# Units of 64 queries instead of 32 in a banded attention, with the global keys apart and the turns moved to transposing transfers

## The chip, the cores and the metric

The kernel runs on one core of one Trainium2 chip. The time is device microseconds of the whole launch. The core has five engines that run their own instruction streams and meet only at semaphores: TensorE (PE; its weight loads are listed apart as PEld), VectorE (DVE), ScalarE (ACT), GpSimdE (POOL) and SyncE (SP). Transfers are carried by 16 DMA engines; here POOL's queue brings the inputs in, and SP's queue moves data within the chip's memory, turns it, and stores the output. PE reads operands from the on-chip memory of 128 partitions and writes to PSUM, which has eight banks of 512 float32 a partition; all eight are in use.

## What is computed

There are 8 batches of 8 heads, 512 local and 32 global tokens each, with a head dimension of 64. A global query attends to all 544 tokens. A local query attends to the 32 global tokens and to the local ones at most 32 positions away. The result, 4352 rows of 512, goes through two matrices of 512 x 2048 and 2048 x 512 with a hard-swish between them ("MoE" in the names, though there is one expert).

```python
window = 32
s_g   = scale * q_g @ concat(k_g, k_l).T          # global queries: everything
out_g = softmax(s_g) @ concat(v_g, v_l)
s_ll  = where(|i - j| <= window, scale * q_l @ k_l.T, -1e9)
s_lg  = scale * q_l @ k_g.T
out_l = softmax(concat(s_lg, s_ll)) @ concat(v_g, v_l)
x = concat(out_g, out_l)                          # (4352, 512)
h = x @ w_in
out = (h * clip(h + 3, 0, 6) / 6) @ w_out
```

## The kernel before

**Work of one tile.** For each batch b and each j of 0 to 3, `local_step` handles 128 queries of all 8 heads.

- Score (L741, L748): the 128 queries are cut into 4 units of 32. A unit sees 96 local keys, so the score of a head is 32 global columns and 96 local ones, 128 in all. The global part takes 8 matmuls of a full 128*128 array with 32 columns (L741; `kgz` holds the global keys of a head pair with zeros for the other head). The local part takes 32 matmuls on pieces of 64*32 of the array, 96 columns each (L748). All 8 heads fill two PSUM banks, `s`.
- Softmax: per head, DVE adds the mask, scales, takes the extreme (L763) and ACT takes the exponential with its sum (L774). DVE then takes reciprocals (L785) and scales in two halves (L789) into `pn`, 8 x 128 columns of float16.
- Turn: `pn` is turned into `et`, keys on the partitions. In batches 0 to 3 PE does it (L797) by 8 transposing matmuls into the bank `t`, and DVE or ACT copies that out; from batch 4 on (`TURN_E = 4`) SP issues a transposing transfer (L808).
- AV (L830): 16 matmuls of a full array with 64 columns, each for one unit and two heads. Their weights are V "strips" in `st`: for every unit, 32 rows of global V and 96 rows of local V on one set of partitions. Seven SP transfers a batch build them (`strips_moved`, L624). Batch 0 (`NEAR = 1`) does without strips and uses 6 groups of smaller pieces instead (`av_near`, L822).
- Evacuation: two copies of 64 partitions each (L410 on ACT, L412 on DVE) from the banks `a` to `xt`, the second after the first.

**Other steps.** Loads of q and k are turned to `qk` by PE (L677) up to batch 4 and by a transfer (L667) from batch 5 on (`TURN_QK = 5`). The global queries of a batch take one score (L865, 64*32 pieces, in the banks of `s` and `a` together), a softmax into two `pg` of 640 columns, two turns of five matmuls on PE (L904), and an AV of 20 matmuls (L918). The MoE part is `first` (L941, matmuls into one of three banks `m`, ACT L948, DVE L952) and `second` (L964, an evacuation, and a store by SP, L981). Its matmuls have 512 columns, except in batches 0 and 1, where `first` works on 128 or 256 tokens at a time.

**What sets the order.** Nothing is scheduled on the chip. A planner in the kernel (`Plan.lay`) holds every step with its engine, an assumed duration and a sort key, and lays them out in time, with rings of buffers and a model of the two DMA queues; `RANKS` shifts the key of single steps. The instructions are issued in the order of the planned starts, and each engine runs its own list strictly in that order. Up to batch 1's first AV (`NEAR` before, 1 after), the planner also puts filler matmuls (L1093) into planned gaps of PE, which keep it busy.

Of the kernel before, what the change touches and what calls it, by code (L numbers as in the profile page):

```python
# [8 lines left out]
FP32 = mybir.dt.float32  # L9
# [13 lines left out]
    ('first', 0, 0, 0): -5.75, ('first', 0, 0, 1): 0.67, ('first', 0, 0, 2): 0.4, ('first', 0, 0, 3): 6.76,  # L23
    ('first', 0, 1, 0): 0.4, ('first', 0, 1, 1): 1.43, ('first', 0, 1, 2): -4.6, ('first', 0, 1, 3): -0.17,
    ('first', 0, 2, 0): -0.94, ('first', 0, 2, 1): -0.54, ('first', 0, 2, 2): -20.75, ('first', 0, 2, 3): -5.21,
    ('first', 1, 0, 0): -1.01, ('first', 1, 0, 1): -23.76, ('first', 1, 0, 2): -0.6, ('first', 1, 0, 3): 0.03,
    ('first', 1, 1, 0): 0.85, ('first', 1, 1, 2): -0.63, ('first', 1, 1, 3): 21.84, ('first', 2, 0, 0): -17.92,
    ('first', 2, 0, 1): 0.44, ('first', 2, 0, 2): -21.92, ('first', 2, 0, 3): 0.52, ('first', 3, 0, 1): 0.09,
    ('first', 3, 0, 2): -0.07, ('first', 3, 0, 3): 0.03, ('first', 4, 0, 0): -27.07, ('first', 4, 0, 1): -13.96,
    ('first', 4, 0, 2): -38.28, ('first', 4, 0, 3): -23.15, ('first', 5, 0, 0): -12.9, ('first', 5, 0, 1): -13.16,  # L30
    ('first', 5, 0, 2): -2.15, ('first', 5, 0, 3): 0.54, ('first', 6, 0, 0): -20.42, ('first', 6, 0, 1): -21.28,
    ('first', 6, 0, 2): -0.07, ('first', 6, 0, 3): -18.08, ('first', 8, 0): 0.87, ('first', 8, 1): -0.2,
    ('first', 8, 2): -0.03, ('first', 8, 3): 1.73,
    ('gav', 0): -13.93, ('gav', 1): 12.35, ('gav', 2): 6.1, ('gav', 3): -1, ('gav', 4): 1.99, ('gav', 5): -7.53,
    ('gav', 6): 3.03, ('gav', 7): 3.5,
    ('gscore', 0): -0.3, ('gscore', 1): -0.5, ('gscore', 2): -2.91, ('gscore', 3): 0.71, ('gscore', 4): -0.1,
    ('gscore', 5): 2.75, ('gscore', 6): 13.26, ('gscore', 7): 25.36,
    ('gsoft', 0): -1.87, ('gsoft', 1): 1.47, ('gsoft', 2): 1.59, ('gsoft', 3): -1.64, ('gsoft', 4): 0.79,
    ('gsoft', 5): 1.77, ('gsoft', 7): -0.1,
    ('gturned', 0): -28.89, ('gturned', 1): -12.61, ('gturned', 2): -4.03, ('gturned', 3): -2.33,  # L40
    ('gturned', 4): 0.6, ('gturned', 5): 4.12, ('gturned', 6): 3.37, ('gturned', 7): -6.87,
    ('keys', 1): -1.63, ('keys', 2): -0.33, ('keys', 3): 5.83, ('keys', 4): -0.3, ('keys', 7): 3.91,
    ('load', 0, 'g'): 1.15, ('load', 0, 'h'): -0.15, ('load', 0, 'v', 0): 0.54, ('load', 0, 'v', 1): -0.1,
    ('load', 0, 'v', 2): 0.3, ('load', 0, 'v', 3): 0.76, ('load', 0, 'v', 4): 1.12, ('load', 0, 0, 0): -0.22,
    ('load', 0, 0, 1): -0.3, ('load', 0, 1, 0): 0.89, ('load', 0, 1, 1): 3.09, ('load', 0, 2): -0.06,
    ('load', 0, 3): 0.76, ('load', 1, 'v', 0): 3.07, ('load', 1, 'v', 1): 4.91, ('load', 1, 'v', 3): 3.42,
    ('load', 1, 'v', 4): 5.23, ('load', 1, 0): 1.79, ('load', 1, 1): 0.76, ('load', 1, 2): 1.79,
    ('load', 1, 3): 2.27, ('load', 2, 'g'): -0.2, ('load', 2, 'v', 0): 3.39, ('load', 2, 'v', 1): 2.09,
    ('load', 2, 'v', 2): 1.05, ('load', 2, 'v', 3): 0.37, ('load', 2, 'v', 4): 4.22, ('load', 2, 0): 3.39,
    ('load', 2, 1): 2.67, ('load', 2, 2): 1.54, ('load', 2, 3): -0.03, ('load', 3, 'v', 0): 2.17,  # L50
    ('load', 3, 'v', 1): 0.06, ('load', 3, 'v', 2): -0.97, ('load', 3, 'v', 3): 1, ('load', 3, 'v', 4): 4.07,
    ('load', 3, 0): 2.8, ('load', 3, 1): 1.41, ('load', 3, 2): 1.31, ('load', 3, 3): 2.5, ('load', 4, 'g'): 3.96,
    ('load', 4, 'v', 0): -2.18, ('load', 4, 'v', 1): -0.3, ('load', 4, 'v', 2): 2.86, ('load', 4, 'v', 3): 0.6,
    ('load', 4, 'v', 4): -1.81, ('load', 4, 0): 5.52, ('load', 4, 2): 1.29, ('load', 4, 3): 0.96,
    ('load', 5, 'v', 0): 4.13, ('load', 5, 'v', 1): 8.46, ('load', 5, 'v', 2): 12.41, ('load', 5, 'v', 3): 3.46,
    ('load', 5, 'v', 4): 4.75, ('load', 5, 0): 12.72, ('load', 5, 1): 17.91, ('load', 5, 2): 3.86,
    ('load', 5, 3): 7.2, ('load', 6, 'g'): 0.17, ('load', 6, 'v', 0): 0.64, ('load', 6, 'v', 1): 6.46,
    ('load', 6, 'v', 2): 15.64, ('load', 6, 'v', 3): 6.5, ('load', 6, 'v', 4): 5.97, ('load', 6, 0): 0.5,
    ('load', 6, 1): 47.7, ('load', 6, 2): 0.03, ('load', 6, 3): -6.89, ('load', 7, 'v', 0): -5.4,
    ('load', 7, 'v', 1): -3.6, ('load', 7, 'v', 2): -2.3, ('load', 7, 'v', 3): -9.19, ('load', 7, 'v', 4): -2.87,  # L60
    ('load', 7, 0): 24.13, ('load', 7, 1): 16.14, ('load', 7, 2): 24.5, ('load', 7, 3): 18.29,
    ('scale', 0, 0): -16.01, ('scale', 0, 1): -5.01, ('scale', 0, 2): 1.29, ('scale', 0, 3): -35.33,
    ('scale', 1, 0): -0.04, ('scale', 1, 1): 2.47, ('scale', 1, 2): -3.97, ('scale', 1, 3): 1.16,
    ('scale', 2, 0): 0.3, ('scale', 2, 1): -3.59, ('scale', 2, 2): -2.23, ('scale', 2, 3): -0.73,
    ('scale', 3, 0): 5.95, ('scale', 3, 1): -0.03, ('scale', 3, 2): -2.15, ('scale', 3, 3): -0.03,
    ('scale', 4, 0): -2.42, ('scale', 4, 1): 3.51, ('scale', 4, 2): 0.2, ('scale', 4, 3): 2.27,
    ('scale', 5, 0): 0.27, ('scale', 5, 1): -3.93, ('scale', 5, 2): -1.76, ('scale', 5, 3): -3.01,
    ('scale', 6, 0): -0.33, ('scale', 6, 1): 0.27, ('scale', 6, 2): 2.07, ('scale', 6, 3): 0.27,
    ('scale', 7, 0): 0.51, ('scale', 7, 1): -1.99, ('scale', 7, 2): 0.25, ('scale', 7, 3): 10.31,
    ('score', 0, 0): 5.87, ('score', 0, 1): -0.66, ('score', 0, 2): 3.85, ('score', 0, 3): 1.13,  # L70
    ('score', 1, 1): -0.27, ('score', 1, 2): -4.39, ('score', 1, 3): -0.3, ('score', 2, 0): -0.3,
    ('score', 2, 1): 2.89, ('score', 2, 2): 0.1, ('score', 2, 3): -12.27, ('score', 3, 0): 1.88,
    ('score', 3, 1): 1.72, ('score', 3, 2): 0.64, ('score', 3, 3): 9.74, ('score', 4, 0): -3.93,
    ('score', 4, 1): -4.05, ('score', 4, 2): 1.04, ('score', 4, 3): -0.71, ('score', 5, 0): -0.48,
    ('score', 5, 1): -0.3, ('score', 5, 2): 4.12, ('score', 5, 3): 1.41, ('score', 6, 0): -1.63,
    ('score', 6, 1): 13.99, ('score', 6, 2): 6.98, ('score', 6, 3): 9.74, ('score', 7, 0): 11.38,
    ('score', 7, 1): 16.28, ('score', 7, 2): 13.94, ('score', 7, 3): 16.91,
    ('second', 0, 0): 0.3, ('second', 0, 1): 0.08, ('second', 0, 2): -3.22, ('second', 0, 3): 0.08,
    ('second', 1, 0): -0.32, ('second', 1, 1): -1.02, ('second', 1, 2): 0.28, ('second', 1, 3): 1,
    ('second', 2, 0): 0.39, ('second', 2, 1): 0.69, ('second', 2, 2): 0.97, ('second', 2, 3): -0.76,  # L80
    ('second', 3, 0): -0.11, ('second', 3, 1): -0.43, ('second', 3, 2): 1.19, ('second', 3, 3): -0.27,
    ('second', 4, 0): 6.42, ('second', 4, 1): 7.47, ('second', 4, 2): 5.52, ('second', 4, 3): -0.13,
    ('second', 5, 0): 15.37, ('second', 5, 1): 11.1, ('second', 5, 2): 14.56, ('second', 5, 3): -1.03,
    ('second', 6, 0): 60.42, ('second', 6, 1): 28.72, ('second', 6, 2): 48.59, ('second', 6, 3): 13.46,
    ('second', 7, 0): 3.75, ('second', 7, 1): 38.92, ('second', 7, 2): 23.81, ('second', 7, 3): 30.25,
    ('second', 8, 0): 1.26, ('second', 8, 1): 2.54,
# [1044 lines left out]
```

## Time and profile before

| | |
|---|---|
| Median of 3 runs | 330.6 us (329.19 to 332.8) |
| Profiled execution | 330.47 us, its span 328.7 us |
| Granted PE clock, mean | 0.995 |
| Busy: PE, DVE, ACT, POOL | 317.9, 264.4, 249.1, 105.6 us |
| MoE matmuls L964 and L941, busy | 128.4 and 120.1 us |
| Fillers, L1093 | 28 |
| Turns of `et` and `qk` by transfer | 16 and 12, 4.9 us to land (median) |
| `st` strips, transfers per batch | 7 (384, 512, 256 and 128 KB) |

Matmuls are pipelined, so the lengths of single matmuls overlap, and busy PE is not PE at its peak. What a step costs is the distance from its first start to the start of what follows. The DMA share is the mean busy share of the 16 DMA engines in a stretch, and is above 1 where two queues have packets in flight on the same engine. Idle time of an engine that is not the bottleneck costs nothing.

### The profile page before, as it was taken

How to read it: one execution, taken by the hardware profiler on the slowest of the kernel's cores; microseconds unless marked ns; L12 is line 12 of the kernel's file. 1: busy time of each engine (PE TensorE's matmuls, PEld its weight loads, DVE VectorE, ACT ScalarE, POOL GpSimd, SP SyncE). 2: the span in 40 equal slices, each digit the busy share in tenths (PEclk: the TensorE clock that was granted, in tenths of full speed). 3: DMA queues.
4: the chain of work that ended last, by engine and by line, in shares of the span. 5: the costliest groups of instructions: out<-in, count | busy, mean ns of one | idle time of the engine just before them, and what ended most of it. 6: DMA issues, size and time to landing. Idle time of an engine off the chain costs nothing.

```text
span 328.7 us, 10251 instructions
## 1 busy us (share of the span) xinstructions
PE 317.9 (97%) x3892; PEld 190.7 (58%) x3892; DVE 264.4 (80%) x972; ACT 249.1 (76%) x787; POOL 105.6 (32%) x139
## 2 busy tenths in 40 slices
PE   8799899999999999999899999999999999999996
PEld 4478795678676555645445545554545545448453
DVE  6999999889979999898899799576987997377100
ACT  4789899879968889886888798587977894466121
POOL 8849626962870962137600500041000000000000
PEclk9979999999999999999999999999999999999999
DMA  9999999999999999399999999969753313100032
GB/s 161 174 190 171 197 281 176 159 200 235 194 155 245 178 206 203 47 136 190 205 191 253 165 224 201 198 106 183 185 130 98 35 27 103 59 7 0 3 97 96
DMA packets 152898, 49.83 MB, mean 152 GB/s; under 512 B 137936, under 2 KB 145936, under 8 KB 152848
## 3 DMA queue, kind: packets, MB, share of 16 engines
q0 software_dynamic: 106560, 17.05, 69.9%
q1 hardware_dynamic: 46288, 32.12, 42.5%
q8 instruction: 30, 0.49, 0.6%
q14 instruction: 20, 0.16, 0.1%
HBM read 35.19 MB, written 8.91 MB: 134 GB/s over the span
## 4 chain that ended last, share of the span: by engine, by line
PE 79%; DVE 10%; DMA 5%; ACT 3%; issue 1%; SPq 0%; ACTq 0%
PE m L964 34%; PE m L941 30%; PE a L830 4%; DVE sm L763 3%; DMA et<-pn 2%; PE s L748 2%; DVE gs L952 2%; PE t L797 2%; DMA st<-ve 2%; ACT sm L774 2%; PE a L822 1%; PE t L677 1%; PE s L741 1%; DMA st<-in_q_l_dram 1%; DVE pn L789 1%
## 5 line engine op out<-in xcount | busy, mean ns | idle before, releaser
L964 PE MATMUL m<-wout,gs 128*128 128x512 f16 (+1 forms) x560 | 128.4, 373 | 0.0
L941 PE MATMUL m<-xt,win 128*128 128x512 f16 (+2 forms) x704 | 120.1, 321 | 1.2 <-DVE gs L952 0.7
L774 ACT ACTIVATE sm<-sm,stat 128x128 f32<-128x128 f32 x256 | 100.0, 393 | 13.9 <-DVE stat L763 13.3
L952 DVE SCALAR_TENSOR_TENSOR gs<-t,m 128x512 f16<-128x512 f32 x136 | 91.0, 683 | 14.6 <-ACT t L948 13.9
L941 PEld LDWEIGHTS <-win 128*128 128x128 f16 x768 | 68.3, 98 | 47.9 <-issue 2.8
L948 ACT ACTIVATE t<-m 128x512 f32<-128x512 f32 x136 | 80.1, 594 | 19.8 <-PE m L941 18.9
L964 PEld LDWEIGHTS <-gs 128*128 128x128 f16 x560 | 51.2, 98 | 50.8 <-issue 1.1
L763 DVE CUSTOM_DVE_ANT_0 sm<-s,mask 128x128 f32<-128x128 f32 x256 | 60.0, 283 | 3.9 <-PE s L748 3.4
L774 ACT ACTIVATION_READ_ACCUMULATOR sm<-sm,stat 128x1 f32 x256 | 48.8, 191 | 0.0
L505 POOL DMA_DIRECT2D ve<-in_v_l_dram x40 | 32.7, 828 | 43.3 <-PE a L918 32.4
L789 DVE TENSOR_TENSOR pn<-sm,stat 128x512 f16<-128x512 f32 x64 | 44.0, 688 | 1.1
L410 ACT CAST xt<-a 64x512 f16<-64x512 f32 x55 | 31.7, 577 | 15.9 <-PE a L830 14.1
L505 POOL DMA_DIRECT2D nat<-in_q_l_dram x30 | 27.5, 916 | 30.6 <-PE t L677 15.1
L505 POOL DMA_DIRECT2D nat<-in_k_l_dram x30 | 27.4, 913 | 8.7 <-DMA wout<-in_moe_w_out_dram 5.3
L410 ACT COPY ot<-m 128x512 f32<-128x512 f32 (+1 forms) x21 | 11.8, 562 | 19.3 <-PE m L964 19.1
L763 DVE DVE_READ_ACCUMULATOR2_ANT stat<- 128x1 f32 x256 | 21.0, 82 | 0.0
L830 PEld LDWEIGHTS <-st 128*128 128x128 f16 x448 | 16.6, 98 | 6.4 <-issue 1.8
L830 PE MATMUL a<-et,st 128*128 128x64 f16 x448 | 17.7, 193 | 1.6 <-DMA et<-pn 1.6
L505 POOL DMA_DIRECT2D ve<-in_v_g_dram x8 | 4.9, 608 | 30.3 <-PE a L918 30.3
L785 DVE RECIPROCAL stat<-stat 128x4 f32<-128x4 f32 x64 | 10.9, 172 | 3.5 <-ACT sm L774 2.9
L412 DVE COPY ot<-m 128x512 f32<-128x512 f32 x14 | 9.6, 686 | 5.0 <-PE m L964 5.0
L741 PEld LDWEIGHTS <-qk 128*128 128x128 f16 x224 | 9.4, 96 | 4.9 <-issue 0.4
(86 smaller groups left out, 274.3 us busy)
## 6 DMA issues: line engine op xcount, KB each, us to landing
out_dram<-ot SPq DMA_DIRECT2D x31, 256.0 KB, 3.7
st<-ve SPq DMA_DIRECT2D x14, 384.0 KB, 8.2
nat<-in_q_l_dram POOLq DMA_DIRECT2D x30, 128.0 KB, 6.3
nat<-in_k_l_dram POOLq DMA_DIRECT2D x30, 128.0 KB, 6.5
st<-ve SPq DMA_DIRECT2D x7, 512.0 KB, 8.6
st<-ve SPq DMA_DIRECT2D x14, 256.0 KB, 7.6
ve<-in_v_l_dram POOLq DMA_DIRECT2D x24, 128.0 KB, 5.9
win<-in_moe_w_in_dram POOLq DMA_DIRECT2D x4, 512.0 KB, 9.6
```

The costliest lines, as they stand in the source:

```text
L410: nc.scalar.copy(out=out, in_=in_)
L505: nc.gpsimd.dma_start(out=dst(op), in_=src)
L741: nc.tensor.matmul(out=ps[:, e, p * P:p * P + G], lhsT=lhs, rhs=kgz[r][:, p, e, :])
L763: nc.vector.tensor_tensor_reduce(out=sm[sm_op.slot][:, h, :], in0=psS[s.slot][:, e, p * P:(p + 1) * P], in1=m, scale=-scale, scalar=3.0e38 ...
L774: nc.scalar.activation(out=sm[sm_op.slot][:, h, :], in_=sm[sm_op.slot][:, h, :], func=EXP, scale=-1.0, bias=stat[stat_op.slot][:, 0, h:h + 1],
L785: nc.vector.reciprocal(out=stat[stat_op.slot][:, 2, h0:h1], in_=stat[stat_op.slot][:, 1, h0:h1])
L789: (nc.gpsimd if op.eng == "POOL" else nc.vector).tensor_tensor(out=pn[pn_op.slot][:, h0:h1, :], in0=sm[sm_op.slot][:, h0:h1, :], in1=stat[ ...
L830: nc.tensor.matmul(out=ps[:, p // 2, c0:c0 + 64], lhsT=st[r][:, u * NJ + j, p * P:(p + 1) * P], rhs=et[et_op.slot][:, 2 * p:2 * p + 2, u * ...
L941: nc.tensor.matmul(out=psM[op.slot][:, i * n:(i + 1) * n], lhsT=w_in_t[:, m, (c + i) * P:(c + i + 1) * P], rhs=x()[:, m, t0:t0 + n], start ...
L948: nc.scalar.activation(out=t1[to.slot], in_=psM[f.slot], func=RELU, bias=0.5, scale=1.0 / 6.0)
L952: nc.vector.scalar_tensor_tensor(out=gs[set_.slot][:, c:c + k, t0:t0 + n], in0=t1[to.slot].rearrange("f (k t) -> f k t", k=k), scalar=1.0, ...
L964: nc.tensor.matmul(out=psM[(f or op).slot][:, a * n:(a + 1) * n], lhsT=gs[set_.slot][:, c, t0:t0 + P], rhs=w_out_t[:, c, a * n:(a + 1) * n ...
```

## The change

A unit is now 64 queries, which see 128 local keys. The 32 global columns are kept apart, so a head's score is 160 columns wide (`KW`), and the 8 heads take three PSUM banks; AV takes one where it had two.

- Score: the last head's local part comes first, as 4 pieces of 64*32; then the 8 global matmuls; then 14 matmuls of 64*64 with 128 columns.
- The softmax works on 160 columns a head. The scaling of the global columns is an operation of its own (`sc_g`); it packs the 8 heads into two further blocks of `pn` (10 blocks instead of 8).
- AV: 4 full matmuls of 128 columns take the global part, with `vgz` as weights, which holds the global V of four heads block by block with zeros elsewhere; then 16 matmuls on half arrays (128 rows, 64 columns of weights) with 64 columns take the local part, one per unit and head. Their weights are plain V (`ve`) for the first unit of a tile and V shifted by 64 rows (`st`) for the second. There are no strips: two transfers a batch build the shifted V. Four small loads a batch build `vgz`.
- Batch 0 takes the same path as the others; `av_near` and half of the masks go.
- The evacuation of AV is one copy of 128 partitions.
- `TURN_QK` goes from 5 to 2, `TURN_E` from 4 to 1, and the turns of `pg` go to transfers from batch 2 on (`TURN_G = 2`). All are issued by SP.
- `ve` has three buffers instead of two. The first clearing of buffers is cut in two, and the single-precision q and k of the start have their own buffer.
- All `RANKS` are new, and the assumed durations of the changed steps. In the built instruction order there are 63 fillers instead of 28.

```diff
-    NEAR = 1
+    QP = 2 * UQ
+    NQ = P // QP
+    KW = P + G
...
-    NS, NX, VE = 2, 3, 2
-    psS = many(1, [P, 2, 512], FP32, "s", pp)
+    NS, NX, VE = 2, 3, 3
+    scored = pp.tile([P, 4, 512], FP32, tag="s", name="s")
+    psS, psA = [scored[:, 0:3, :]], [scored[:, 3, :]]
...
-    psA = many(1, [P, 2, 512], FP32, "a", pp)
...
+    def load_vg(b, key):
+        plan.at = "load", b, "vg"
+        deps = [av_last[b - 2, j] for j in range(NJ)] if b >= 2 else [cleared(b)]
...
+        return [load(lambda op, k=k: vgz[b % 2][k * G:(k + 1) * G].rearrange("g (a m) (c d) -> g a m c d", a=2, c=2)[
+            :, :, k // 2, k % 2, :], v_g[b].rearrange("(a m) g d -> g a m d", a=2)[:, :, k, :], 2 * G, key + 0.001 * k, deps)
+            for k in range(4)]
+
+    def strips(b, key):
...
+            for a in range(2):
+                deps = [x for j in js for x in vload[b, j + a]] + [cleared(b)] + before
+                dst, src = st[r][a * QP:(a + 1) * QP, j0:j1, :], ve[b % VE][(1 - a) * QP:(2 - a) * QP, j0 + a:j1 + a, :]
...
+                    z = add("SP", 600, lambda op, dst=dst, src=src: nc.sync.dma_start(out=dst, in_=src), deps,
+                            key=key + 0.001 * a, dma=(QP, *LONG))
...
-    TURN_QK, TURN_E, TURN = 5, 4, (64, 382.0, 1.9)
+    TURN_QK, TURN_E, TURN_G, TURN = 2, 1, 2, (382.0, 1.9)
...
+            def local(h, n):
+                p, rows = h // 2, slice(h % 2 * D, (h % 2 + 1) * D)
+                for u in range(NQ):
+                    k0 = j * P + u * QP
+                    for q in range(u * QP, (u + 1) * QP, n):
+                        nc.tensor.matmul(out=head(ps, h)[q:q + n, 0:P], lhsT=qk[r][rows, 0, p, UQ + j * P + q:UQ + j * P + q + n],
+                                         rhs=qk[r][rows, 1, p, k0:k0 + P])
+
+            local(H - 1, UQ)
+            for h in range(H):
+                nc.tensor.matmul(out=head(ps, h)[:, P:KW], lhsT=qk[r][:, 0, h // 2, UQ + j * P:UQ + (j + 1) * P],
+                                 rhs=kgz[r][:, h // 2, h % 2, :])
+            for h in range(H - 1):
+                local(h, QP)
...
+        def sc_g(op):
+            nc.vector.tensor_tensor(
+                out=pn[pn_op.slot][:, H:H + 2, :].rearrange("q a (h g) -> q (a h) g", g=G), in0=sm[sm_op.slot][:, :, P:KW],
+                in1=stat[stat_op.slot][:, 2, :].unsqueeze(2).to_broadcast([P, H, G]), op=ALU.mult)
+        scs.append(add("DVE", 330, sc_g, recs, key=key - 0.1, rel=[sm_op, stat_op]))
...
         def av(op):
-            ps = psA[op.slot]
+            ps, w = psA[op.slot].rearrange("d (p q) -> d p q", p=NP), et[et_op.slot]
             for p in range(NP):
-                for u in range(NU):
-                    c0 = (p % 2) * 256 + u * 64
-                    nc.tensor.matmul(out=ps[:, p // 2, c0:c0 + 64],
-                                     lhsT=st[r][:, u * NJ + j, p * P:(p + 1) * P],
-                                     rhs=et[et_op.slot][:, 2 * p:2 * p + 2, u * UQ:(u + 1) * UQ])
+                nc.tensor.matmul(out=ps[:, p, :], lhsT=vgz[r][:, p, :], rhs=w[:, H + p // 2, :], start=p == 0, stop=False)
+            for u, x in enumerate((ve[b % VE], st[r])):
+                for h in range(H):
+                    e, q = h % 2, slice(u * QP, (u + 1) * QP)
+                    nc.tensor.matmul(out=ps[e * D:(e + 1) * D, h // 2, q], lhsT=x[:, j, h * D:(h + 1) * D], rhs=w[:, h, q],
+                                     start=False, stop=u == NQ - 1 and h >= H - 2)
...
+        def xa(op):
+            copy(op, xt[xt_op[b].slot][:, :, j * P:(j + 1) * P], psA[v.slot].rearrange("k (p q) -> k p q", p=NP))
+        return [add(BOTH, (470, 610), xa, [v, xt_op[b]], key=key - 0.5, rel=[v])]
...
+            def move(op, e=e, po=po):
+                nc.sync.dma_start_transpose(out=eg[eg_op.slot][:, e], in_=pg[po.slot])
+            if b < TURN_G:
+                t = add("PE", 281, tr, [c], key=key + 0.2 * e - 0.1, acq="T", rel=[po], cols=640, ins=2 * NV)
...
+                evs.append(add("SP", 1250, move, [c, eg_op], key=key + 0.2 * e - 0.1, rel=[po], dma=(8 * NV, *TURN)))
```

More of the change, by code (lines that the diff above doesn't have):

```diff
@@ L394 @@
     ident = sb.tile([P, P], FP16, tag="ident", name="ident")
[L395 removed]
+    masks = many(3, [P, KW], FP32, "mask")
     w_in_t = sb.tile([P, NP, dff], FP16, tag="win", name="win")
@@ L441, in c @@
-            nc.vector.tensor_copy(out=masks[3], in_=m)
-            nc.vector.memset(masks[3][0:UQ, 0:UQ], OUTSIDE)
-        z = add("DVE", 1450, c, [z], key=-9)
-        def later(after):
-            def full(k, src, rows_, cols, key, deps):
-                z = add(BOTH, (300, 250), lambda op: copy(op, masks[k], src), deps, key=key)
-                return add("DVE", 85, lambda: nc.vector.memset(masks[k][rows_, cols], OUTSIDE), [z], key=key)
-            last = full(5, m, slice(P - UQ, P), slice(P - UQ, P), -1.5, [z, after])
-            zs = [add(BOTH, (280, 250), lambda op, u=u: copy(op, w[u * UQ:(u + 1) * UQ, G:P], m[0:UQ, 0:KL]),
-                      [z, after], key=-1.3) for u in range(NU)]
-            prep["last"] = last
-            prep["masks"] = [full(0, w, slice(0, UQ), slice(G, 2 * G), -1.1, zs),
-                             full(2, w, slice(P - UQ, P), slice(P - UQ, P), -1.1, zs)]
@@ L455, in mask_steps, with last @@
-        prep["later"] = later
+            nc.vector.tensor_copy(out=m[QP:P, 0:P], in_=m[0:QP, 0:P])
+            nc.vector.tensor_copy(out=masks[0], in_=m)
+            nc.vector.memset(masks[0][0:QP, 0:UQ], OUTSIDE)
+        z = add("DVE", 600, c, [z], key=-9)
+        def last():
+            nc.vector.tensor_copy(out=masks[2], in_=m)
+            nc.vector.memset(masks[2][QP:P, P - UQ:P], OUTSIDE)
+        prep["last"] = lambda after: add("DVE", 350, last, [z, after], key=-1.3)
         return z
@@ L471, with clear @@
     nc.scalar.copy(out=kgz[0].rearrange("k p e g -> k (p e g)"), in_=idle[:, 0:NP * 2 * G])
-    def clear():
-        for r in range(2):
+    def clear(first):
+        for r in (0,) if first else (1,):
             for p in range(NP):
@@ L477, in clear, with cleared @@
                 nc.vector.memset(qk[r][:, 1, p, KC - UQ:KC], 0.0)
-        for v in ve:
+            nc.vector.memset(vgz[r], 0.0)
+        for v in ve[:1] if first else ve[1:]:
             nc.vector.memset(v[:, NJ, :], 0.0)
-        nc.vector.memset(kgz[1], 0.0)
-        for r in range(NEAR):
-            nc.vector.memset(st[r][:, NJ:NJ + 2, :], 0.0)
+        if not first:
+            nc.vector.memset(kgz[1], 0.0)
+    def cleared(b):
+        return prep["clear"][min(b, 1)]
     def clear_pg():
@@ L732, in pe @@
         def pe(op):
             ps = psS[op.slot]
-            for p in range(NP):
-                for e in range(2):
-                    lhs = qk[r][:, 0, p, UQ + j * P:UQ + (j + 1) * P]
-                    if near:
-                        nc.tensor.matmul(out=ps[:, e, p * P:(p + 1) * P].rearrange("q (a k) -> q a k", k=G)[:, 0:NU:NU - 1, :],
-                                         lhsT=lhs, rhs=kgz[r][:, p, e:e + 1, :].to_broadcast([P, 2, G]))
-                    else:
-                        nc.tensor.matmul(out=ps[:, e, p * P:p * P + G], lhsT=lhs, rhs=kgz[r][:, p, e, :])
@@ L799, in local_step, with tr, ev @@
         if b < TURN_E:
-            t = add("PE", 447, tr, scs, key=key - 0.2, acq="T", rel=[pn_op], cols=1024, ins=2 * H)
-            et_op = add("DVE", 0, lambda op: None, [t], key=key - 0.3, acq="et")
-            def ev(op):
-                copy(op, et[et_op.slot].rearrange("k h q -> k (h q)"), psT[t.slot])
-            e_ = add(BOTH, (900, 600), ev, [et_op], key=key - 2, rel=[t])
+            et_op, e_ = None, []
+            for a, (lo, hi) in enumerate(((0, H), (H, H + 2))):
+                def tr(op, lo=lo, hi=hi):
+                    for h in range(lo, hi):
+                        nc.tensor.matmul(out=psT[op.slot][:, (h - lo) * P:(h - lo + 1) * P], lhsT=pn[pn_op.slot][:, h, :],
+                                         rhs=ident, is_transpose=True)
+                n = hi - lo
+                t = add("PE", 56 * n, tr, scs if a else scs[:2], key=key - 0.2, acq="T", rel=[pn_op], cols=P * n, ins=2 * n)
+                if a == 0:
+                    et_op = add("DVE", 0, lambda op: None, [t], key=key - 0.3, acq="et")
+                def ev(op, lo=lo, hi=hi, t=t):
+                    copy(op, et[et_op.slot][:, lo:hi, :].rearrange("k h q -> k (h q)"), psT[t.slot][:, 0:(hi - lo) * P])
+                e_.append(add(BOTH, (900, 600) if n == H else (300, 200), ev, [t, et_op], key=key - 2, rel=[t]))
```

410 lines of the change are left out of this document (168 added, 242 removed), and 13 rows, old and new, of the table RANKS.

## The prediction

> **What bounds the kernel now.** I read the page's busy row first, then the stretches, the waits, and the order of time on TensorE (PE). The busy row:
>
> ```profile
> PE 317.9 (97%) x3892; PEld 190.7 (58%) x3892; DVE 264.4 (80%) x972; ACT 249.1 (76%) x787; POOL 105.6 (32%) x139
> ```
>
> PE is busy for 97% of the span of 328.7 us. The same by stretches (length, then busy time of PE, PEld, DVE, ACT, POOL, the granted clock, DMA share, GB/s):
>
> ```profile
> 0.00:20.00 20.00, 15.97 (x194) 9.66 (x194) 16.44 (x86) 12.48 (x47) 15.97 (x27) 0.95 1.53 174
> 20.00:40.00 20.00, 18.66 (x409) 16.22 (x407) 19.00 (x67) 17.40 (x53) 14.88 (x20) 0.96 1.89 179
> 40.00:57.20 17.20, 16.80 (x265) 12.69 (x265) 16.30 (x75) 16.22 (x60) 7.22 (x9) 1.00 1.45 231
> 57.20:285.00 227.80, 225.98 (x2797) 129.35 (x2796) 196.53 (x724) 185.21 (x600) 67.57 (x85) 1.00 1.20 162
> ```
>
> Up to 57.2 us, where batch 1's first AV starts, PE idles 4.0 + 1.3 + 0.4 = 5.8 us; from there to 285 us only 1.8 us in 228. So there a microsecond of PE work is a microsecond of the end. Of the waits, this is the only one of PE for a transposing transfer:
>
> ```profile
> PE a L830 <- DMA et<-pn: 1.6, 1, 1.6
> ```
>
> What a step costs PE is read from successive starts, since the printed lengths overlap (start, length, engine, line, operation, tiles, array shape, operands, count):
>
> ```profile
> 22.41 0.61 PE L822 MATMUL a<-et,st 128*128 128x128 f16 x8
> 22.95 0.29 PE L822 MATMUL a<-et,ve 64*128 64x64 f16 x4
> 23.07 0.28 PE L822 MATMUL a<-et,st 64*128 64x64 f16 x4
> 23.28 0.28 PE L822 MATMUL a<-et,ve 32*128 32x64 f16 x4
> ...
> 189.25 0.35 PE L741 MATMUL s<-kgz,qk 128*128 128x32 f16 x8
> 189.53 0.36 PE L748 MATMUL s<-qk 64*32 64x96 f16 x32
> 189.83 0.39 PE L941 MATMUL m<-xt,win 128*128 128x512 f16 x1
> ...
> 203.08 0.63 PE L830 MATMUL a<-et,st 128*128 128x64 f16 x16
> 203.55 2.75 PE L964 MATMUL m<-wout,gs 128*128 128x512 f16 x12
> 206.23 0.19 PE L865 MATMUL s<-gt 64*32 64x32 f16 x1
> ...
> 206.29 0.37 PE L865 MATMUL a<-qk,gt 64*32 64x512 f16 x1
> 206.60 3.63 PE L964 MATMUL m<-wout,gs 128*128 128x512 f16 x16
> ...
> 210.53 0.44 PE L904 MATMUL t<-ident,pg 128*128 128x128 f16 x5
> 210.81 1.03 PE L964 MATMUL m<-wout,gs 128*128 128x512 f16 x4
> 211.67 0.44 PE L904 MATMUL t<-ident,pg 128*128 128x128 f16 x5
> ```
>
> Three prices follow. A 512-column matmul costs (211.67 - 210.81)/4 = 0.216 us, a 128-column turn 0.28/5 = 0.056, a 64-column AV matmul (203.55 - 203.08)/16 = 0.029. A local score costs 189.83 - 189.25 = 0.58. And **a change of array shape costs 0.09 us**: 203.55 + 12 x 0.216 = 206.14, the 64*32 matmul starts at 206.23; 206.29 + 0.216 = 206.51, the 128*128 one starts at 206.60; 22.41 + 8 x 0.056 = 22.86, the 64*128 one starts at 22.95. Four matmuls into 64*128, 23.07 + 0.12 = 23.19, the next shape starts at 23.28.
>
> **Removed: turns on PE.** Batches 1 to 3 lose 4 turns each of et (8 x 0.056 = 0.45 us): -5.4. Batches 2 to 4 lose 4 turns of qk: -5.4. Batches 2 to 7 lose two turns of pg of 0.28: -3.4. Together **-14.2 us**.
>
> **Scores.** Now: 0.58 = two changes (0.18) + four rounds of 96 columns, eight matmuls abreast (4 x 0.04 = 0.16) + 0.24 for the eight global ones. After: four matmuls 64*32, eight 128*128, fourteen 64*64, then MoE again: four changes (0.37), 0.05 for the first four at 128 columns abreast, 0.24, and fourteen 128-column ones four abreast (3.5 x 0.054 = 0.19): 0.85. Bounds: 0.45 if no change costs anything and the global ones fall to 0.2; 1.04 if the 64*64 ones run two abreast. I take 0.85, made of rows: 28 x 0.27 = **+7.6** for batches 1 to 7.
>
> **AV.** Now 0.47 without a change. After: four full matmuls (0.22), a change, sixteen 64-column ones on half arrays 128*64, a change (0.19 for both). No row shows 128*64. If both halves run abreast at 0.029 a round, 0.23 and in all 0.64; if one waits for the other, 0.46 and 0.88; without changes 0.45. I take 0.04 a round, between the two and what a round of the other column-split shape (64*32) takes: 0.73. 28 x 0.26 = **+7.3**.
>
> [...]
>
> **Batch 0 and the fillers.** Scores 4 x (0.85 - 0.62) = +0.9 (13.59 to 14.21 us in the order of time); AV 4 x (0.73 - 1.45) = -2.9, where 1.45 is 22.41 to the 23.86 of the next MoE matmul; two more turns a tile +0.45: -1.5. But the built instruction order holds 63 filler matmuls where it had 28, all before batch 1's first AV, and issues that AV after 12 matmuls of L964 instead of 24: the start has less PE work and still has to wait. Fillers run whether needed or not: 35 x 0.23 = +8.0. What they may take out of the present 5.8 us of idling is 0 to 5.8; I take 3: **+5**. The start cannot be much shorter, as DVE (19.0 of 20 us) and ACT are full in it: per tile DVE gains 8 x 0.034 (32 more elements at 1.05 ns, from the xg and xt copies, 285 ns for 128 and 689 for 512) plus 0.42 for the new scaling, 0.7 us.
>
> **What hides behind PE.** Over all, DVE gains 256 x 0.034 + 32 x 0.42 = 22 us and loses some 22 in evacuations (et, qk, eg, xt) and masks; ACT loses some 16, as an xt copy of all 128 partitions replaces two of 64: both stay below PE. DMA: strips fall from 2.0 to 0.5 MB a batch (-10.8 MB in seven), turns add 24 transfers of 256 and 320 KB, 12 of 160, and grow 16 others (+9.9 MB): level. A transposing transfer took 4.9 us to land (median), 7.9 at most; by the order, a tile's AV stands 12 to 22 us of PE work behind its score, before as after. SP issues each turn in 1.25 us (median of L808), 36 more make 45 us of its 329, and 49 strip transfers fall to 14. Behind a late one wait SP's stores and later turns, then AV and the MoE matmuls behind it on PE; if that cover goes, it costs what the rival below does. POOL gets 28 small loads of V (some 0.6 us each, as v_g's row of 0.608 has it) that wait for the AVs of two batches before, and what is queued behind them are later loads; POOL is busy 32% of the time and waits now, in the same way, 62.8 us for the global AVs. The evacuation of AV, one copy of 0.58 us where two stood one behind the other, frees the only AV bank 0.6 us sooner. I cost all of this at nothing.
>
> **Sum.** -14.2 + 7.6 + 7.3 - 1.5 + 5 = +4.2 us on 328.7, and 1.8 around the span (330.47 - 328.7): **335 us**. The profiled time is the median's (330.6) within 0.1 us. 1% is about what a measurement here can tell from no change.
>
> **Rivals.** *Weights bound the half arrays*: AV 0.88, 32 x 0.15 = +5 us, 340; for it, no row of such rounds; against it, 64*32 runs eight abreast. Chance 0.15. *Free change to half arrays*: the rows change row split, or both; if splitting columns alone costs nothing and rounds are 0.029, AV is 0.45, -9 us: 326. Chance 0.17, half of it beyond 1%. *Faster, outright*: if none of the added changes costs its 0.09 us (a score 0.45, AV 0.45): 32 x (0.40 + 0.28) = 22 us less, 313. It decides from 0.04 us a change down. Against it: each of the four kinds of change shown costs the same 0.09. Chance 0.10. *Turns come late*: 64 transfers for 28, most in the first 150 us where DMA share is 1.2 to 1.9. If each of the 16 tiles of batches 1 to 4 waits once like L830 above (1.6 us, half of it new), +13: 348. It decides once landing passes the 12 us of slack. Chance 0.13. The forecast keeps 0.45, and holds from 329 to 340 for its fillers (+2 to +8) and its AV rounds; two fifths of it lie within 1%.
>
> So faster 0.10 + 0.08 = 0.18; same 0.09 + 0.18 = 0.27; slower 0.27 + 0.15 + 0.13 = 0.55. The range leaves out the outright gain and the far end of late turns: 323 to 347.
>
> **What would show it.** Score starts 0.85 apart from what follows, AV 0.65 to 0.85, each change 0.09; PE above 96%; batch 1's first AV at 58 to 61 us; waits of PE for et or qk transfers under 3 us. A score of 0.5 us, or gaps of PE longer than 1 us at AV, would make it wrong.

## The result, and the profile after

The changed kernel takes **350.1 us** (median of 4 runs, 349.62 to 352.12) against 330.2 for the kernel before in the same session (329.19 to 332.8): a ratio of 1.060 (95% interval 1.053 to 1.068), slower. The forecast was 335.0 with a range from 323 to 347. The sign was right and the size wrong: the time lies 3 us above the range. Some executions were slower at a lower granted clock (of the last kernel of the experiments, one took 349.68 us at 0.98, the others 342.54 to 344.2 at 0.995 to 1.0); the medians and ratios here leave them out.

The profiled execution has a span of 347.9 us. Its busy row, and the same stretches as before (length, then busy time and instructions of PE, PEld, DVE, ACT, POOL, granted clock, DMA share, GB/s), the last one cut at 59.95 us, in batch 1's first AV:

```profile
PE 327.8 (94%) x3299; PEld 181.5 (52%) x3299; DVE 262.5 (75%) x968; ACT 236.6 (68%) x750; POOL 121.0 (35%) x167
```

```profile
0.00:20.00 20.00, 17.31 (x158) 9.75 (x159) 12.25 (x66) 9.26 (x26) 16.24 (x27) 1.00 1.52 170
20.00:40.00 20.00, 17.91 (x280) 13.44 (x279) 17.64 (x73) 17.87 (x64) 12.54 (x16) 1.00 1.83 181
40.00:59.95 19.95, 18.22 (x260) 13.47 (x258) 17.86 (x67) 17.20 (x53) 15.20 (x23) 1.00 1.64 175
59.95:285.00 225.05, 215.61 (x2185) 112.73 (x2184) 185.97 (x684) 163.02 (x539) 77.01 (x103) 0.99 1.44 155
```

Before, PE idled 1.8 us in the 228 us that follow batch 1's first AV. Now it idles 9.4 in 225. That stretch was the one in which the forecast said "a microsecond of PE work is a microsecond of the end"; after the change it is a stretch of waits.

What the steps cost PE is again read from successive starts (start, length, operation):

```profile
146.66 0.39 PE L791 MATMUL s<-et,vgz 128*128 128x128 f16 x4
146.97 0.32 PE L795 MATMUL s<-et,ve 128*64 128x64 f16 x8
147.12 0.29 PE L795 MATMUL s<-et,st 128*64 128x64 f16 x8
147.35 1.04 PE L928 MATMUL m<-wout,gs 128*128 128x512 f16 x4
...
149.12 2.76 PE L928 MATMUL m<-wout,gs 128*128 128x512 f16 x12
151.81 0.24 PE L704 MATMUL s<-qk 64*32 64x128 f16 x4
151.98 0.37 PE L709 MATMUL s<-kgz,qk 128*128 128x32 f16 x8
152.28 0.41 PE L704 MATMUL s<-qk 64*64 64x128 f16 x14
152.62 1.04 PE L928 MATMUL m<-wout,gs 128*128 128x512 f16 x4
```

An AV is 147.35 - 146.66 = 0.69 us (forecast 0.73). A score is 152.62 - 151.81 = 0.81, and the twelve matmuls ahead of it end at 149.12 + 12 x 0.216 = 151.71, which leaves another 0.10 for the change into the first shape: 0.90 to 0.91 in all (forecast 0.85). So the prices of PE's steps were right to 0.05 us. Taken over the whole trace, I call **stall** what the distance from one matmul's start to the next has beyond the median distance of that pair of shapes, counted where it is over 50 ns (a lowered clock counts in). It is 11.9 us before and 25.4 after. So of the 19.2 us that the span gained, some 13 are stalls and some 6 are work (where the line is drawn moves both by a few us); the forecast's own work terms with all 8 us of the fillers come to +7.2. What was missed are the waits. The only transfer that PE's list names (microseconds in total, times, longest):

```profile
PE s L791 <- DMA et<-pn: 5.0, 4, 1.9
```

DVE's waits of the softmax were, before, for scores alone:

```profile
DVE sm L763 <- PE s L748: 3.4, 3, 2.4
```

Now they are:

```profile
DVE sm L728 <- ACT xt L416: 15.8, 14, 2.8
...
DVE sm L728 <- PE s L795: 12.1, 13, 2.4
DVE sm L728 <- PE s L704: 5.9, 11, 1.3
```

The reader should stop at the first two. L728 reads scores (L704). Line L795 is AV, and L416 the copy of AV's result into `xt`. Nothing in the computation makes the softmax of one tile wait for the AV of another. It waits because scores and AV now are slices of one PSUM tile (`scored`, four banks), and the framework's waits hold for a whole tile. The instructions of L728 carry 59 waits after the change, 22 of them on ACT and 37 on PE; those of the same step before (L763) carry 32, 31 of them on PE and none on ACT.

### The profile page after: what moved, and what is told of

The parts are those of the page before. It is cut to its first block, busy times and chain, and to the rows that moved or that the text cites. A ratio compares the mean times of both kernels' runs of the same rounds, so it can differ in the third digit from the quotient of the medians.

```text
span 347.9 us, 9127 instructions
## 1 busy us (share of the span) xinstructions
PE 327.8 (94%) x3299; PEld 181.5 (52%) x3299; DVE 262.5 (75%) x968; ACT 236.6 (68%) x750; POOL 121.0 (35%) x167
## 3 DMA queue, kind: packets, MB, share of 16 engines
q1 hardware_dynamic: 81152, 31.17, 54.7%
## 4 chain that ended last, share of the span: by engine, by line
PE 70%; DMA 14%; DVE 11%; ACT 4%; issue 1%; ACTq 0%; DVEq 0%
PE m L905 29%; PE m L928 23%; DMA et<-pn 14%; DVE sm L728 6%; PE s L704 4%; PE s L1053 3%; PE s L795 3%; PE s L709 2%; PE s L791 2%; PE s L882 1%; DVE gs L916 1%; ACT xt L416 1%; DVE pn L755 1%; PE m L550 1%; ACT sg L846 1%
## 5 line engine op out<-in xcount | busy, mean ns | idle before, releaser
L739 ACT ACTIVATE sm<-sm,stat 128x160 f32<-128x160 f32 x256 | 107.0, 420 | 20.4 <-DVE stat L728 19.9
L728 DVE CUSTOM_DVE_ANT_0 sm<-s,mask 128x160 f32<-128x160 f32 x256 | 69.8, 319 | 35.9 <-ACT xt L416 15.8
L416 ACT CAST xt<-s 128x512 f16<-128x512 f32 x27 | 15.8, 586 | 24.8 <-DVE stat L728 11.8
L498 POOL DMA_DIRECT2D vgz<-in_v_g_dram x28 | 15.1, 547 | 49.1 <-PE s L791 43.4
L704 PE MATMUL s<-qk 64*64 64x128 f16 (+1 forms) x576 | 20.9, 226 | 4.3 <-DVE stat L728 2.3
L416 ACT COPY ot<-m 128x512 f32<-128x512 f32 (+1 forms) x22 | 12.4, 564 | 17.8 <-PE m L928 17.7
L728 DVE DVE_READ_ACCUMULATOR2_ANT stat<- 128x1 f32 x256 | 21.2, 83 | 0.0
L704 PEld LDWEIGHTS <-qk 64*64 64x64 f16 (+1 forms) x576 | 11.5, 103 | 15.5 <-issue 8.2
L791 PE MATMUL s<-et,vgz 128*128 128x128 f16 x128 | 12.5, 219 | 6.7 <-DMA et<-pn 5.0
L846 ACT ACTIVATE sg<-s,stat 128x544 f32<-128x544 f32 x16 | 11.4, 713 | 9.6 <-DVE stat L838 8.0
L791 PEld LDWEIGHTS <-vgz 128*128 128x128 f16 x128 | 9.3, 97 | 15.5 <-issue 3.3
```

The lines of the kernel that those rows point to most:

```text
L416: nc.scalar.copy(out=out, in_=in_)
L498: nc.gpsimd.dma_start(out=dst(op), in_=src)
L704: nc.tensor.matmul(out=head(ps, h)[q:q + n, 0:P], lhsT=qk[r][rows, 0, p, UQ + j * P + q:UQ + j * P + q + n], rhs=qk[r][rows, 1, p, k0:k0 + P])
L728: nc.vector.tensor_tensor_reduce(out=sm[sm_op.slot][:, h, :], in0=head(psS[s.slot], h), in1=m, scale=-scale, scalar=3.0e38, op0=ALU.add, o ...
L739: nc.scalar.activation(out=sm[sm_op.slot][:, h, :], in_=sm[sm_op.slot][:, h, :], func=EXP, scale=-1.0, bias=stat[stat_op.slot][:, 0, h:h + 1],
L791: nc.tensor.matmul(out=ps[:, p, :], lhsT=vgz[r][:, p, :], rhs=w[:, H + p // 2, :], start=p == 0, stop=False)
```

## The experiments

Times are medians; "over before" is the distance to the kernel before, run on the same chip in the same session. A plain copy in place of a turn leaves the data unturned, so such a kernel's output is not the attention's and only its time is read.

| kernel | us | over before | ratio, 95% interval |
|---|---|---|---|
| changed kernel | 350.1 | +19.9 | 1.053 to 1.068 |
| two PSUM tiles | 342.6 | +11.7 | 1.030 to 1.045 |
| turns as plain copies | 344.9 | +14.1 | 1.038 to 1.046 |
| both | 331.6 | +0.2 | 0.9998 to 1.0034 |
| fewer changes of shape | 347.4 | +16.5 | 1.046 to 1.056 |
| no fillers | 352.1 | +21.2 | 1.060 to 1.069 |

### Two PSUM tiles instead of one

The instruction order stays; scores get a tile of three banks, AV one of its own. The global score, which used all four, is packed into three.

```diff
-    scored = pp.tile([P, 4, 512], FP32, tag="s", name="s")
-    psS, psA = [scored[:, 0:3, :]], [scored[:, 3, :]]
+    psS = many(1, [P, 3, 512], FP32, "s", pp)
+    psA = many(1, [P, 512], FP32, "a", pp)
```

> The changed kernel with the same instruction order, but the score banks and the AV bank are two PSUM tiles instead of slices of one (the global score moves into the three score banks, with its last four small matmuls in one more array shape, and one scaling in two pieces: some +1 us). Theory A, one shared tile makes every reader and writer of scores, AV and their evacuation wait for each other: 4 to 8 us of PE idling go, 343 to 347 us, and DVE's first operation on a score no longer waits for AV or its evacuation. Theory B, the added loss is only the late landing of turns: 349 to 352 us, PE idle unchanged at 20 us.

342.6 us (341.31 to 346.33). The waits of the softmax (now L729) for AV and for its copy are gone; its only long wait is for scores (L705), in the trace of an execution of 346.3 us:

```profile
DVE sm L729 <- PE s L705: 16.4, 15, 2.9
```

So the shared tile is a cause, and its removal alone is worth 19.9 - 11.7 = 8.2 us (by the distances over before). The stalls at AV, 8.5 us before this edit, are 8.9 after it: there is a second cause.

### Turns as plain copies

All 64 transposing transfers become plain transfers of the same bytes between the same tiles, at the same place; the lines for `et` are shown, `qk` and `pg` change likewise.

```diff
-                nc.sync.dma_start_transpose(out=et[op.slot], in_=pn[pn_op.slot].rearrange("q h k -> q (h k)"))
+                nc.sync.dma_start(out=et[op.slot], in_=pn[pn_op.slot])
```

> The changed kernel with the same instruction order, but the 64 transposing transfers are plain copies of the same bytes between the same buffers, so the data is not turned (the output is that of unturned data). Theory B, the turns land late because they are transposing transfers of 256-byte packets beside the loads: et lands in about 5 us instead of 8.7, AV waits less, 342 to 346 us. Theory A: landing may fall, but the time stays within 348 to 351 us.

344.9 us (343.97 to 345.1). `et` lands 3.5 us after its issue (median) instead of 8.7, the loads of q 6.3 instead of 8.9, and the stalls at AV fall from 8.5 to 3.1 us. The bytes are the same, but not what they cost. The row of SP's queue (packets, MB, share of 16 engines' time) is, in the changed kernel and then with plain copies:

```profile
q1 hardware_dynamic: 81152, 31.17, 54.7%
```

```profile
q1 hardware_dynamic: 41728, 31.17, 32.1%
```

### Both

> The two earlier edits together: scores and AV in two PSUM tiles, and the 64 transposing transfers as plain copies of the same bytes (what they leave is unturned, so the output is not the attention's). Alone they took 7.5 and 5.2 us off the changed kernel. If the shared tile and the late turns are two separate costs, they add up: 337.4 us, ratio 1.020, with PE idle under 13 us and AV's stalls for et under 4 us. If both remove the same idle time of PE, the time stays near 341 us, ratio 1.032.

331.6 us (330.87 to 332.47), where the sum of the two savings promised 337.4: **the whole loss is gone**, and PE's stalls are 7.4 us, less than the 11.9 of the kernel before. The last stretch, cut at 59 us here, idles 0.6 us:

```profile
59.00:285.00 226.00, 225.36 (x2319) 120.13 (x2317) 196.80 (x730) 170.47 (x567) 76.41 (x102) 1.00 1.06 160
```

Read from this end, late turns alone cost 11.7 - 0.2 = 11.5 us, the shared tile alone 14.1 - 0.2 = 13.9, and both 19.7, not 25.4. They overlap. The waits above suggest how: an AV that waits for `et` also holds the tile which the next softmax wants, and a softmax that waits for an AV issues its `et` late. Whoever removes only one of them sees about half of what it costs alone: 8.2 of 13.9 us, 5.8 of 11.5.

### The shared tile in the kernel before

```diff
-    psS = many(1, [P, 2, 512], FP32, "s", pp)
+    scored = pp.tile([P, 4, 512], FP32, tag="s", name="s")
+    psS, psA = [scored[:, 0:2, :]], [scored[:, 2:4, :]]
...
-    psA = many(1, [P, 2, 512], FP32, "a", pp)
```

> The kernel before with its scores and its AV in one PSUM tile of four banks, nothing else changed: the shared tile alone. With no turn late, two tiles instead of one were worth 344.9 - 331.6 = 13.3 us in the changed kernel; if the wait costs by itself, this is 336 to 345 us here. If it costs only beside late turns and the new softmax of 160 columns, within 2 us of before.

350.9 us (348.99 to 352.02), +19.8, ratio 1.058 (1.049 to 1.066). One part of the change alone, two lines for two, with the order of instructions the same on every engine (only waits are added), costs the old kernel as much as the whole change did. The same two waits appear (L822 is batch 0's AV, L410 the copy):

```profile
DVE sm L763 <- ACT xt L410: 11.3, 15, 3.0
DVE sm L763 <- PE s L822: 5.8, 3, 2.4
```

### Which turns are late

Each kernel has two PSUM tiles. Plain are: only `et`; only `qk` and `pg`; only the 12 `et` of batches 1 to 3.

> Two PSUM tiles and only the 28 turns of et as plain copies (the output is not the attention's); those of qk and pg turn as in the changed kernel. With all turns 342.6 us, with none 331.6. If AV waits because the turning of et itself is slow, et is what counts: 332 to 334 us, et landing near 4 us. If the turns make one another and the loads late (they share the transfers' engines), the 36 others keep their part: 336 to 339 us, and et, though plain, lands later than the 3.5 us it took with none turning.

> The counterpart: two PSUM tiles, the 24 turns of qk and 12 of pg as plain copies (the output is not the attention's), et turned by transfers as in the changed kernel. If et's own turning is what is slow: 339 to 342 us and et still at 8 us or more. If it is the sum of turning traffic: 335 to 338 us, et landing between 4.5 and 6.5 us.

> Two PSUM tiles, and only the twelve et transfers of batches 1 to 3 as plain copies (their output is not the attention's); the sixteen of batches 4 to 7 and all of qk and pg turn. With all et turning 342.6 us, with all plain 332.1. If the twelve moved ones are the cost, 332 to 335 us; if those of batches 4 and 5, which were transfers before, are late too, 336 to 340.

Only `et` plain: 332.1 us (+1.3, 1.002 to 1.007). Only `qk` and `pg` plain: 340.3 (+9.5, 1.027 to 1.034). The twelve: 336.1 (+5.6, 1.012 to 1.021). So the 36 turns of `qk` and `pg` cost the end 1 to 2 us by being turned in transfer, and the 28 of `et` 9 to 10: 6.1 for the twelve that PE used to make (11.7 - 5.6), 4.3 for the others (5.6 - 1.3). With `qk` and `pg` plain, `et` still takes 9.1 us to land: the turns of the others are not what makes it late. The landings by stretch (57 to 180 us, then 180 to 330), of the kernel before:

```profile
et<-pn SPq DMA_TRANSPOSE x5, 6.4
...
et<-pn SPq DMA_TRANSPOSE x12, 3.8
```

and after:

```profile
et<-pn SPq DMA_TRANSPOSE x14, 9.7
...
et<-pn SPq DMA_TRANSPOSE x13, 5.6
```

In the kernel with both causes away, AV starts 7.3 to 15.3 us behind the issue of its `et` in batches 1 to 3 (each tile's two starts in the trace), and in six of the twelve tiles under 9.7. So the median landing of 9.7 is already too late for half of them. In batches 4 and 5 it is too late for three of eight.

### AV placed later

Two PSUM tiles, the score in three shape changes, and the order changed so that AV stands at least 9, or 10.5, planned us behind the issue of `et`; what depends on it moves along.

```diff
+    for (b, j), v in av_last.items():
+        if (b, j) in behind:
+            place[v] = (max(v.start, behind[b, j] + 9000), v.n)
```

> Two PSUM tiles, the score with three changes of shape instead of four, and the instruction order changed so that the AV of a tile stands at least 9 planned us behind the issue of its et transfer (7 to 10 us as measured, 6.1 and more as planned, in batches 1 to 5); what depends on it moves along. The whole computation. If et is late because this distance is shorter than its landing of 9.4 to 9.7 us, PE's stalls for et fall from 9 to 11.5 us to under 4, and the time from some 340 to 342 us to 331 to 335. If the turning disturbs in another way (loads late, clock), it stays within 2 us of 341.

> The same with 10.5 planned us. By the distance theory the stalls for et are all but gone, and the time is 328 to 333 us unless MoE's first matmuls now wait for the later AV (two thirds of the AVs move by 1 to 5 us); by the other theory 341 us or more.

354.0 us (+22.9, 1.058 to 1.079; two executions) and 366.0 (+34.9, 1.097 to 1.113). The wait itself went as the distance theory says: at AV, PE stalls 2.1 us with 10.5, where two PSUM tiles alone left 8.9. But the times lie 19 and 33 us above what was expected for that theory. The largest wait of PE is now that MoE's `first` (L910), which moved behind the later AV, waits for the hard-swish of its own banks:

```profile
PE m L910 <- DVE gs L921: 13.6, 14, 2.6
```

Stalls ahead of `first` are 22 us; the rest of the 34.9 was not taken apart. Distance for `et` is not free in this order; it would have to be planned.

### Fewer changes of shape

The score's global part comes first, in the shape that MoE leaves, then 64\*64, then 64\*32; all three kernels also put AV's global part on half arrays (not shown). The first has nothing else changed, the second also has two PSUM tiles, the third two tiles and plain copies.

```diff
-            local(H - 1, UQ)
             for h in range(H):
                 nc.tensor.matmul(out=head(ps, h)[:, P:KW], ...
-            for h in range(H - 1):
+            for h in (H - 1, *range(H - 2)):
                 local(h, QP)
+            local(H - 2, UQ)
```

> The changed kernel with the same order of steps, but each score starts with its global part and ends with four 64*32 pieces (three changes of array shape instead of four), and AV's global part runs on half arrays too (one change instead of two): by 0.093 us a change and 0.05 for what runs beside, 0.24 us a tile, 7.6 us over 32 tiles. If PE's work sets the end: 342 to 345 us. If waits set it: 348 to 350 us, and PE idles longer.

> Two PSUM tiles, and fewer changes of array shape (score three instead of four, AV one instead of two). The shapes alone took 6.5 us of PE work away and only 2.7 us of time. If it was the shared tile that turned PE's gain into waits, the 6.5 us now come through: 342.6 - 6.5 = 336 us, ratio 1.018. If the turns that arrive late set AV, PE waits for et instead: 340 us, ratio 1.030, with AV's stalls for et above 11 us (9.0 with two tiles and the old shapes).

> Two PSUM tiles, all 64 turns as plain copies of the same bytes (what they leave is unturned, so the output is not the attention's), and fewer changes of array shape: 6.5 us of PE work less than the kernel of two tiles and plain copies (331.6 us), which idles only 6 us. If it is bound by PE's work, as the forecast took the kernel to be, the 6.5 us come through in full: 325 us, ratio 0.981. If something behind PE takes over, about what the shapes gave with all waits in place, 2.7 us: 329 us.

A miscount stands in all three: AV gained nothing (0.69 as before: half arrays still need a change in and one out, and I had credited the first to the step ahead of it). The score fell from 0.90 to 0.79 us between neighbouring MoE matmuls, so PE's work fell by 32 x 0.11 = 3.5 us, not 6.5. By the distances over before, it gave 3.4 us alone (347.4, +16.5), nothing with two tiles (343.7, +12.3, 1.033 to 1.047; stalls at AV 12.3 us instead of 8.9), and 1.8 with two tiles and plain copies (329.1, -1.6, 0.994 to 0.997). The intervals of the first two reach 0.5% and more to each side, so only the third step is clear of noise. There about half of the saved work reaches the end; whether waits for transfers swallow it elsewhere is not shown.

### No fillers

> The changed kernel without its 63 filler matmuls. If they stand where PE has to wait anyway: 348 to 352 us. If they cost what my prediction charged (5 us): 344 to 346 us. If PE's clock falls without them: above 352 us, with the granted clock under 0.9 in the first 60 us.

352.1 us (351.75 to 352.18; `fill` returns the steps alone). In this kernel the 63 fillers cost nothing: batch 1's first AV starts at 59.61 us without them and at 59.67 with them. They stand where PE would wait anyway.

### Turns back on PE

By the planner: two PSUM tiles, all key shifts zero (the planner finds no order with the shifts of either kernel when turns change engines), turns as after the change, and turns as before it.

```diff
-        o = Op(eng, dur, emit, deps, key + RANKS.get(self.at, 0.0), acq, rel, 0, dma)
+        o = Op(eng, dur, emit, deps, key + 0.0 * RANKS.get(self.at, 0.0), acq, rel, 0, dma)
...
-    TURN_QK, TURN_E, TURN_G, TURN = 2, 1, 2, (382.0, 1.9)
+    TURN_QK, TURN_E, TURN_G, TURN = 5, 4, 8, (382.0, 1.9)
```

> Two PSUM tiles and all shifts of keys at zero, so the planner lays the order by its plain keys: the ground for the next kernel. No theory gives its time to better than 345 to 375 us, as the shifts were chosen for another order; what counts is its distance from the next one.

> The same with the turns of qk, et and pg by PE as long as in the kernel before (batches 0 to 4, 0 to 3 and all), 36 turns back on PE, the order laid by plain keys. They cost PE 14.2 us (at 0.056 us for 128 columns, et's now ten blocks instead of eight: 15.5) and some 20 us more of copies on DVE and ACT. If the transfers pay what the forecast took off, this is 10 to 15 us slower than the kernel without shifts just above. If late turns give most of it back, it is 0 to 5 us slower; if the transfers cost more than PE's turns, it is faster.

354.9 us (+23.5, 1.066 to 1.080) and 353.0 (+21.6, 1.063 to 1.072): no difference that can be told. PE is busy for 339.3 us with its own turns and for 327.0 with transfers; in this order those 12 us of work come back in full as waits.

In the order of the change, without the planner (two tiles and the score in three changes in each): `qk` of batches 2 to 4 by PE at the place where the transfer was issued; `et` of batches 1 to 3 likewise; nine of these twelve in two parts with their copies behind.

> Two PSUM tiles, fewer changes of shape, and the 12 turns of qk of batches 2 to 4 back on PE at the place in the order where the transfer was issued: the whole computation. PE gets 12 x 0.45 = 5.4 us of work and DVE and ACT some 10 us of copies. Against two tiles and fewer changes (343.7 us): if the 12 transfers cost by making et late, PE's waits for et go from 11.5 to under 6 us and the sum is 343.7 + 5.4 - 6 to -10 = 339 to 343 us; if they do no harm, it is 349 us.

> Two PSUM tiles, the score with three changes, and et of batches 1 to 3 turned by PE as in the kernel before, at the place in the order where the transfer was issued: 12 turns of ten blocks, 12 x 0.56 = 6.7 us of PE work, and 12 times some 1.5 us of copies on DVE and ACT. The whole computation. If the twelve late transfers cost more than they saved, it is faster than 341 us: 334 to 339. If PE waits for the softmax at these places instead (as it did with qk turned in place, 351 us), 343 to 350.

> Two PSUM tiles, the score with three changes of shape, and nine of the twelve et of batches 1 to 3 turned by PE again, each in two parts with its copies placed behind it, where the bank for turns is free; the whole computation. PE gets 9 x 0.56 = 5.0 us of work, DVE and ACT some 13 us of copies. If late et costs what the plain copies say (10.5 us of 342.6, most of it in the twelve), it is 341 + 5 - 8 = 336 to 339 us. If the copies on DVE and ACT delay the softmax instead, 342 to 350.

`qk`: 351.2 us (+20.4, 1.055 to 1.068). The same kernel with the transfers is at +12.3, so it is 8.1 worse, more than the 5.4 of PE work: in this order these transfers pay. `et` in place: 363.8 (+32.7). Part of this one's output is not the attention's: it writes its turns to the bank `t` without reserving it, so it probably overwrites what other steps keep there. And it tells little of the turns' price, as PE waits for its own copies between two rounds through one bank:

```profile
PE t L788 <- ACT et L791: 14.0, 12, 1.5
```

Nine in two parts: 343.1 us (+12.6, 1.036 to 1.045), about the time of the transfers (+11.7 and +12.3). Stalls at AV fall to 5.9 us from the 8.9 of two PSUM tiles alone; 5.0 us of PE work and the copies take it back. No version that computes the whole attention came below the kernel before; the nearest is two PSUM tiles, 342.6 us.

## Why the prediction was right and wrong

- **Work on PE: right.** The change of shape at 0.09 us held (here 0.093 into 64\*32 and into half arrays). Score +0.32 instead of +0.27 (28 x 0.05 = 1.4 us more), AV +0.22 instead of +0.26 (1.1 less). The rival of weights that bound the half arrays is out: sixteen matmuls take 147.35 - 146.97 - 0.09 = 0.29 us, 0.036 a round of two halves, and AV is 0.69, not 0.88. The two rivals of free changes are out too, as each change cost its 0.09.
- **Fillers: mis-sized, and the start right by luck.** Batch 1's first AV starts at 59.67 us, inside the forecast of 58 to 61, but with fillers or without. With both waits gone it starts at 55.39, where the forecast's own terms give 57.2 - 12 x 0.216 - 1.5 + 5 = 58.1. So of the "+5" 2.3 were there, and the waits filled the gap. That is most of the 3.4 us by which the kernel without the two waits, 331.6, lies under the forecast.
- **"A transposing transfer took 4.9 us to land (median)" against "12 to 22 us of PE work behind its score": the step that failed for late turns.** The two distances have different starting points. A landing counts from the issue, and between score and issue the softmax takes 6.1 to 15.1 us (in the kernel with both waits gone). What is left from issue to AV is 5.4 to 16.7, median 10.1. And 4.9 is a median over a kernel whose turns mostly ran after 180 us: 3.8 there, 6.4 ahead of it. In the changed kernel, `et` landed at 9.7 ahead of 180 us, where the moved turns are. "DMA: [...] level" was true of bytes and false of time: 17 and 31 to 32 MB in the two queues either way, but SP's queue went from 42.5 to 54.7% of 16 engines' span. The issue was under-priced as well: the forecast took 1.25 us of SP for each turn, and after the change an `et` takes 1.87 and a `qk` 2.64 (median).
- **The rival "turns come late"** (348, chance 0.13) had one of the two mechanisms, but its decision point, 12 us, was measured from the score. That its 348 lies near 350.1 is luck: by the runs late turns are worth 11.5 us alone, some 342, and the shared tile makes up the rest.
- **The wait that was not on the list: the step that failed for the shared tile.** The forecast read `psS, psA = [scored[:, 0:3, :]], [scored[:, 3, :]]` as banks, and credited the single copy of AV with freeing "the only AV bank 0.6 us sooner". It is a merge of two tiles into one, hence new waits of the softmax on AV and its copy: 13.9 us alone, and 19.8 in the kernel before. No row of before shows it, but the diff and the instruction list do.
- **The signs "waits of PE for et or qk transfers under 3 us" and "PE above 96%"**: they came out at 5.0 us and 94%. The longest gap of PE at AV is 1.93 us, over the 1 us that the forecast named as a sign of being wrong.

What stays open is why a turned `et` is slow. In the trace it moves in 1,280 packets of 256 bytes, as a plain copy in 128 of 2,560, so packets and turning changed together. `qk` moves in 1,024 packets of 256 bytes either way, and between 57 and 180 us it lands at 8.6 us turned (with only `et` plain) and 6.7 plain (with all plain). But plain beside a turning `et` it lands at 9.4, so its neighbours count as much as its own turning. Also, a landing counts from the start of the issue, and an `et` holds SP for 1.87 us at its issue, as a plain copy for 0.48 (medians). The shares in `et`'s delay were not measured.

## What to carry to other kernels

When a diff regroups buffers into slices of one tile, ask which instructions now share their waits, and count the waits in the built instruction list; regrouping moved no work and still cost the kernel before 6% by itself. Compare a transfer's landing with the distance from its issue to its first reader, in the stretch where it will run, and price transfers by the queues' share of time, not by bytes: here 31.17 MB took 54.7% of 16 engines' time with turns and 32.1% with plain copies. Two waits that feed each other must be removed together before either is judged.

## What the runs showed of the hardware

One stall of the changed kernel cost twice. After a wait of 2.1 us (184.55 + 12 x 0.216 = 187.14 to 189.24) PE's next 512-column matmuls ran at half rate, (192.63 - 190.96)/4 = 0.418 us each:

```profile
184.55 2.76 PE L928 MATMUL m<-wout,gs 128*128 128x512 f16 x12
189.24 0.38 PE L791 MATMUL s<-et,vgz 128*128 128x128 f16 x4 [1.93 <-DMA et<-pn]
...
190.96 1.89 PE L928 MATMUL m<-wout,gs 128*128 128x512 f16 x4
192.63 1.60 PE L905 MATMUL m<-xt,win 128*128 128x512 f16 x4
```

and the granted clock of the 2 us stretches (the third column from the end) shows it in two of them:

```profile
188.00:190.00 2.00, 0.76 (x24) 0.65 (x24) 0.93 (x2) 0.63 (x4) 1.39 (x2) 1.00 1.46 237
190.00:192.00 2.00, 2.00 (x29) 1.11 (x30) 0.32 (x3) 0.94 (x3) 0.00 (x0) 0.59 2.34 159
192.00:194.00 2.00, 2.00 (x6) 0.70 (x5) 2.00 (x14) 1.39 (x7) 0.00 (x0) 0.56 1.70 178
194.00:196.00 2.00, 2.00 (x11) 0.88 (x9) 1.34 (x6) 1.73 (x6) 0.00 (x0) 1.00 1.95 177
```

That is 2 x 0.41 + 2 x 0.44 = 1.7 us on top of the 2.1. It did not follow every wait: of the six gaps of PE over 1 us between two matmuls of this trace (1.04 to 1.93 us), it came behind this one alone, the longest. Why it came there was not shown.

The other surprise is the price of turning a transfer. Beside the loads, 57 to 180 us, `et` lands at 10.0 us turned and 4.7 plain, both with `qk` and `pg` plain, and the loads of q land at 8.9 and 5.7. The plain `et` also moves in larger packets, 2,560 bytes instead of 256; what part of the difference is the turning was not shown.
